# One matmul over both ends of a ring buffer: the fifth token tile of a fused attention and bilinear feed-forward kernel

## The chip, the cores and the metric

The kernel runs on one core of a Trainium2 chip. The metric is the device time of one execution in microseconds (us). The engines are named as in the profile: PE is TensorE's matrix multiplication and PEld its weight load, DVE is VectorE, ACT is ScalarE, POOL is GpSimd, SP is SyncE, which here only issues DMAs. A name with q behind it (SPq, POOLq) is that engine's instruction queue.

## The reference

Two stages, the second fed by the first. B is 8, H is 8, S is 576 and D is 64, so there are 4608 tokens of width 512; the hidden width is 1536.

```python
scores = np.matmul(q, k.transpose(0, 1, 3, 2)) / np.sqrt(D)
masks = [mask_local if h < H // 2 else mask_strided for h in range(H)]   # a band of 32, or every 32nd key
attn_out = softmax(np.where(masks, scores, -1e9)) @ v
x = attn_out.transpose(0, 2, 1, 3).reshape(B * S, H * D)
out = ((x @ w_a) * (x @ w_b)) @ w_out
```

## The kernel before, in words

**Tiles and slots.** The feed-forward part walks over nine tiles of 512 tokens, t = 0 to 8; the fifth tile is t = 4. A tile has sixteen slots, numbered 16 t + 0 to 16 t + 15. The first twelve (`ffn_ab`, f = 0 to 11) each make one block of 128 hidden columns: the projection a on four 128-row pieces of the width (kk = 0 to 3), then the projection b in the same way, each into a bank of PSUM (`ab_mm`, L617 to L627). ACT copies a into `a_sb` (L647) and DVE multiplies it by b into the tile `pf` (L650). The last four slots multiply `pf` by `w_out`. Tiles 2 to 8 do that with a seven-product scheme on pairs of token groups (`ffn_ys`, `y_plan`, L812), whose sums DVE makes ahead (`fast_s`, L758). For f = 0 the order of kk is 0 and 2, then 1, then 3 (L642), since pieces 1 and 3 of x come last.

**The attention of the next batches** is woven in. Each batch b has 576 tokens, and its steps stand in lists by slot (L584 to L592): S makes scores into a `st` bank (L392), then ACT's exponential and DVE's mask; V multiplies by v into an `o` bank (L470 or L529), after which either DVE normalizes into `xl` rows, or ACT takes a logarithm and an exponential (L538, L539) and DVE multiplies into xT (L545). `take(i)` runs the steps of slot i; `mid` runs those of slot i - 0.5 between a and b.

**The x ring.** xT holds the activations, transposed, in a ring of four batches: XR * S = 2304 columns (L160). Token n lies in column n modulo 2304. Tile t reads columns from 512 t modulo 2304 on. Only for t = 4 does that run over the end: tokens 2048 to 2303 are in columns 2048 to 2303, tokens 2304 to 2559 in columns 0 to 255. `ab_mm` cuts it there (`cuts`, L618 to L619): for t = 4 every projection is two matmuls of 256 columns, each with its own load of the same weights. For every other tile it is one of 512.

**PSUM banks.** The a and b banks and the three banks X, Y, Z of the output stage come from one pool of four (`mm_bank`, L612). A matmul into a bank waits until the engine that read its last content is done.

**SP's queue.** All DMAs of the later attention steps (L346, L350), the two halves of x that go through memory (`rows_out` L511 writes a scratch, `rows_in` L516 reads it back transposed into xT) and the stores of y leave through SP, in program order. `y_plan` stores its tile in two halves, i = 0 and 1, at slots 16 t + 19 and 16 t + 20, that is slots 3 and 4 of the next tile (L821, L822). Half i holds 128 partitions of two rows of 512 float32 values; a partition is (a, s) with a from 0 to 15 and s from 0 to 7, and the output row is 32 a + 16 i + 2 s + q (L806). Each DMA of SP also waits for the DMA that used the same of eight completion semaphores before it, which is the one eight places earlier on SP's queue. The buffers `y_sb` are two per tile, so the output stage of the next tile waits, before its first copy into each (L789), for the store that reads it.

The whole order on PE, DVE, ACT, POOL and SP is the program's own (`manual_schedule`, L905).

Of the kernel before, what the change touches and what calls it, by code (L numbers as in the profile page):

```python
# [31 lines left out]
def kernel(  # L32
# [10 lines left out]
    nc = tc.nc  # L43
    B, H, S, D = q.shape
# [7 lines left out]
    TTOK = 512  # L52
# [106 lines left out]
    XR = 4  # L159
    xT = const.tile([128, KD, XR * S], BF16)  # L160
# [5 lines left out]
    HT = TTOK // 2  # L166
# [437 lines left out]
    def take(pos):  # L604
        for b, names in steps.get(pos, ()):
            run(b, names)
# [5 lines left out]
    def mm_bank(shape):  # L612
        nm = "tp" if used[0] % 4 == 3 and used[0] >= 0 else "mm"
        used[0] += 1
        return psum4[nm].tile(shape, F32, tag=nm, name="mm")

    def ab_mm(t, f, ab, kks, mid=None, first=0, last=KD - 1, ws=(0, 1)):  # L617
        n = min(TTOK, XR * S - TTOK * t % (XR * S))  # L618
        cuts = [(0, n)] + ([(n, TTOK - n)] if n < TTOK else [])  # L619
        for w, ps_ in [((wa_sb, wb_sb)[i], ab[i]) for i in ws]:  # L620
            if mid and ps_ is ab[1]:
                mid()
            for kk in kks:
                for c0, n in cuts:
                    x0 = (TTOK * t + c0) % (XR * S)
                    nc.tensor.matmul(ps_[:, c0:c0 + n], lhsT=w[:, kk, 128 * f:128 * (f + 1)], rhs=xT[:, kk, x0:x0 + n],  # L626
                                     start=(kk == first and c0 == 0), stop=(kk == last and c0 == cuts[-1][0]))  # L627

    def ffn_ab(t, f, mid, ab=None):
        if f == 0:  # L630
            pfs[t] = fsb.tile([128, FD, TTOK], BF16, tag="pf", name="pf", bufs=1)
        pf = pfs[t]
        if f // 2 in FAST_A.get(t, ()):
            if f % 2 == 0:
                pairs[t, f // 2] = a_pair(t, f // 2)
            return next(pairs[t, f // 2])
        if ab is None:
            ab = [mm_bank([128, TTOK]) for _ in range(2)]
            if f == 0:

                late = 1 if t == 1 else 3
                for kks in ((0, 2, 3), (1,)) if t == 1 else ((0, 2), (1,), (3,)):  # L642
                    ab_mm(t, f, ab, kks, last=kks[-1] if kks[-1] == late else -1)
            else:
                ab_mm(t, f, ab, range(KD), mid)
        a_sb = fsb.tile([128, TTOK], F32, tag="a_sb", name="a_sb")
        nc.scalar.copy(a_sb, ab[0])  # L647
        if t in FAST_Y:
            halves = lambda x: x.rearrange("p (a i s) -> p a i s", i=2, s=16)
            nc.vector.tensor_mul(pf[:, f, :].rearrange("p (i a s) -> p a i s", i=2, s=16), halves(a_sb), halves(ab[1]))  # L650
        else:
            nc.vector.tensor_mul(pf[:, f, :], a_sb, ab[1])
        return pf[:1, f, :1]
# [109 lines left out]
    def products(t):  # L763
        pf, s = pfs[t], pss[t]
        full = lambda e, i: (lambda g, q: pf[:, 2 * g + e, HT * i + q:HT * (i + 1):2])
        summed = lambda n: (lambda g, q: s[:, n, g, q:HT:2])
        wsum = lambda n: (lambda g: wf[:, n, g])
        wfull = lambda e, j: (lambda g: wov[:, e, j, g])
        return {"1": ("X", full(0, 0), wfull(0, 0)), "2": ("Y", full(1, 0), wfull(1, 0)), "3": ("X", summed(3), wfull(1, 1)),
                "4": ("Z", full(1, 1), wsum(3)), "5": ("X", summed(0), wsum(0)), "6": ("X", summed(1), wsum(1)),  # L770
                "7": ("Z", summed(2), wsum(2))}
# [8 lines left out]
    def y_bufs():  # L780
        return [fsb.tile([128, 2, d_model], F32, tag="y_sb", name="y_sb", bufs=2) for _ in range(2)]

    def y_post(k, y, q, bank, n=slice(0, HN)):

        part = lambda i, j: y[i][:, q, HN * j:HN * (j + 1)]
        if k == "+":
            nc.vector.tensor_tensor(part(1, 1), part(1, 1), part(0, 1), op=ALU.add)  # L787
        elif k in "1765":
            nc.scalar.copy({"1": part(0, 0), "7": part(0, 1), "6": part(1, 0), "5": part(1, 1)}[k], bank)  # L789
        elif k == "4":  # L790
            nc.vector.tensor_tensor(part(1, 0), bank, part(1, 0), op=ALU.add)
        elif k == "2":
            nc.vector.tensor_tensor(y[0][:, q, n], bank, y[0][:, q, n], op=ALU.add)
        elif k == "3":
            nc.scalar.copy(part(0, 1), bank)
# [4 lines left out]
    def y_plan(t):  # L800

        plan, y = products(t), y_bufs()
        bank = {x: mm_bank([128, 2, HN]) for x in "ZXY"}

        def store_half(i):
            rows = out[TTOK * t:TTOK * (t + 1)].rearrange("(a i s q) c -> a s i (q c)", i=2, s=8, q=2)  # L806
            nc.sync.dma_start(out=rows[:, :, i], in_=y[i].rearrange("p q c -> p (q c)"))

        for n, (k, q) in enumerate(Y_ORDER):
            b, lhs, rhs = plan[k]  # L810
            for g in range(FG):
                nc.tensor.matmul(bank[b][:, q], lhsT=lhs(g, q), rhs=rhs(g), start=k in "172" and q == 0 and g == 0,  # L812
                                 stop=g == FG - 1, skip_group_check=True)
                if g == FG - 1:
                    if q == 1:
                        y_post(k, y, slice(0, 2), bank[b])
                        if k == "5":
                            y_post("+", y, slice(0, 2), None)
                    take(("y", t, n + 1))
                yield y  # L820
        do(16 * t + 19, store_half, 0)  # L821
        do(16 * t + 20, store_half, 1)  # L822
# [82 lines left out]
    with tc.manual_schedule(engines={ENG.PE, ENG.SP, ENG.Pool, ENG.DVE, ENG.Activation}):  # L905
# [11 lines left out]
        for x, src in ((raw[0], k), (raw[1], q)):  # L917
            nc.sync.dma_start(out=x[:96].rearrange("p (h r d) -> p h r d", h=2, d=D),
                              in_=src[0, 0:2].rearrange("h (p r) d -> p h r d", r=RL))
# [15 lines left out]
        first = {}  # L935
        for nm in ORDER:
            if nm[0] == "*":
                spin(int(nm[1:]))
            elif nm == "C0":
                for x, cp, n in ((raw[0], nc.vector.tensor_copy, "k"), (raw[1], nc.scalar.copy, "q")):  # L940
                    t = nats[0, n, False][:, 0:2].rearrange("p h r d -> p (h r d)")
# [5 lines left out]
            elif nm == "M":  # L947
                mask_local2()
            elif nm[0] == "G":
                mask_group(int(nm[1]))  # L950
                if nm == "G1":
                    load_vs(0)
                    for c in range(2):
                        load_w(c)
                    load_w(2)
                    load_qk(1, True, (0, 1))
                    load_qk(1, True, (2, 3))
                    load_vs(1)
                    load_w(3)
                    load_qk(1, False)  # L960
            elif nm == "Z":
                zero_qz(1, nc.scalar, ((0, 0),))
            elif nm[0] == "F":
                f = int(nm[1])
                if nm[2] == "A":
                    if f == 1:
                        ab = pst.tile([128, 2, 512], F32, tag="st", name="ab")
                        first[f] = [ab[:, 0], ab[:, 1]]
                    else:
                        first[f] = [psum4["misc"].tile([128, 512], F32, tag="misc", name="ab")]  # L970
                elif nm == "F0B":
                    first[f].append(psum4["o"].tile([128, 512], F32, tag="o", name="ab"))
                ab_mm(0, f, first[f], {"A": (0, 1), "B": (0, 1), "b": (2,), "c": (3,)}[nm[2]],
                      ws={"A": (0,), "B": (1,)}.get(nm[2], (0, 1)))
            else:
                PART[nm[:-2] + nm[-1]](int(nm[-2]))
# [15 lines left out]
        def do(i, fn, *args):  # L992
            at.setdefault(i, []).append(lambda: fn(*args))
# [99 lines left out]
```

## Time and profile before

| what | value |
|---|---|
| three runs | 325.45, 325.69, 326.91 us; median 325.69 |
| the profiled execution | 325.6 us, of which the span from first to last instruction is 323.9 |
| busy: PE, DVE, ACT, POOL | 317.7, 258.6, 189.4, 161.0 us |
| granted TensorE clock | 1.000 |
| tile 4, from its first matmul to the first of its output stage | 159.49 to 183.47 us |
| tile 5, the same | 193.66 to 217.13 us |

A busy time counts every moment with an instruction of that engine under way. A matmul's recorded duration is longer than the distance to the next one, since matmuls overlap in the array; so distances between starts tell the cost, and durations do not. "Idle before" is the time that an engine stood still ahead of a group, with the releaser that ended most of it. The chain that ended last walks back from the last instruction: at each step to whatever released it, or else to the instruction before it on its engine.

### The profile page before, as it was taken

To read this page: it belongs to the slowest core of one execution; us is meant where nothing else is said; L and a number is where in the kernel's file an instruction comes from. 1 tells how busy PE (TensorE), PEld (TensorE's weight loads), DVE (VectorE), ACT (ScalarE), POOL (GpSimd) and SP (SyncE) were. 2 spreads that over 40 slices of the span, in tenths; PEclk is the share of its full clock that TensorE was granted. 3 is DMA by queue.
4 is the path that set the end of the run, shared out by engine and by line. 5 is a ranking of instruction groups with operands and counts; after the bars stand their busy time and mean duration, and the time that the engine had idled before them with its cause. 6 is when DMAs were issued, how large, how long until landed. Compare 5 with 4: busy or idle time off the path is not lost.

```text
span 323.9 us, 7466 instructions
## 1 busy us (share of the span) xinstructions
PE 317.7 (98%) x2686; PEld 209.2 (65%) x2686; DVE 258.6 (80%) x560; ACT 189.4 (58%) x332; POOL 161.0 (50%) x291
## 2 busy tenths in 40 slices
PE   8999999999999999999999999999999999999994
PEld 6754655455555587557999885569555966686673
DVE  6766888888778899898888888988999768837952
ACT  6764775478764576447644764476546655335541
POOL 8935848599857554853576247634013012203500
PEclk9999999999999999999999999999999999999999
DMA  9999999999999989999999999999146040004004
GB/s 158 151 203 194 204 187 188 170 174 129 141 216 142 134 87 98 111 209 152 101 101 189 176 97 106 175 194 115 33 95 157 10 130 3 0 0 132 1 2 130
DMA packets 110724, 40.43 MB, mean 125 GB/s; under 512 B 88672, under 2 KB 107744, under 8 KB 110688
## 3 DMA queue, kind: packets, MB, share of 16 engines
q0 software_dynamic: 85968, 19.48, 67.0%
q1 hardware_dynamic: 24576, 20.42, 25.1%
q8 instruction: 21, 0.34, 0.5%
q14 instruction: 15, 0.12, 0.1%
q10 hardware_dynamic: 144, 0.07, 0.1%
HBM read 39.51 MB, written 10.91 MB: 156 GB/s over the span
## 4 chain that ended last, share of the span: by engine, by line
PE 95%; DMA 1%; ACT 1%; DVE 1%; issue 0%; SPq 0%
PE mm L626 46%; PE mm L812 17%; PE mm L876 6%; PE mm L710 5%; PE st L392 4%; PE o L470 2%; PE ax L703 2%; PE o L529 2%; PE mm L703 2%; PE mm L841 2%; PE end L841 1%; DMA raw<-in_q_dram 1%; PE misc L155 1%; PE ab L626 1%; PE tp L296 1%; PE tp L554 1%
## 5 line engine op out<-in xcount | busy, mean ns | idle before, releaser
L626 PE MATMUL mm<-xT,wa_sb 128*128 128x512 bf16 (+1 forms) x400 | 92.6, 353 | 0.0
L626 PE MATMUL mm<-xT,wb_sb 128*128 128x512 bf16 (+1 forms) x400 | 92.6, 353 | 0.0
L647 ACT COPY a_sb<-mm 128x512 f32<-128x512 f32 x88 | 51.4, 585 | 51.3 <-PE mm L626 49.3
L626 PEld LDWEIGHTS <-wb_sb 128*128 128x128 bf16 x408 | 39.4, 98 | 35.6 <-DMA wb_sb<-in_moe_w_b_dram 0.2
L1059 POOL CAST pace<-pf 1x1 f32<-1x1 bf16 x83 | 24.7, 298 | 69.0 <-DVE pf L650 48.3
L626 PEld LDWEIGHTS <-wa_sb 128*128 128x128 bf16 x408 | 36.6, 98 | 23.1 <-issue 0.2
L650 DVE TENSOR_TENSOR pf<-a_sb,mm 128x512 bf16<-128x512 f32 x66 | 44.8, 680 | 8.4 <-PE mm L626 7.2
L413 ACT ACTIVATE p<-st 72x576 bf16<-72x576 f32 (+1 forms) x56 | 36.4, 650 | 14.4 <-PE st L392 14.2
L545 DVE TENSOR_TENSOR xT<-o,xr 64x288 bf16<-64x288 f32 x48 | 21.4, 446 | 14.7 <-ACT xr L539 14.4
L812 PEld LDWEIGHTS <-ps 128*128 128x128 bf16 x288 | 28.0, 98 | 3.1
L789 ACT COPY y_sb<-mm 128x512 f32<-128x512 f32 (+1 forms) x28 | 15.5, 555 | 17.9 <-PE mm L812 15.3
L812 PE MATMUL mm<-wf,ps 128*128 128x256 bf16 x216 | 25.5, 273 | 0.0
L538 ACT ACTIVATE xr<-o 64x576 f32<-64x576 f32 x28 | 18.1, 647 | 12.0 <-PE o L529 11.7
L876 PE MATMUL mm<-wo_sb,pf 128*128 128x512 bf16 x96 | 23.4, 379 | 0.0
L243 POOL DMA_DIRECT2D vs<-in_v_dram x24 | 19.6, 818 | 5.0 <-PE mm L812 2.4
L812 PEld LDWEIGHTS <-pf 128*128 128x128 bf16 x216 | 20.3, 98 | 2.5 <-issue 0.2
L1059 POOL COPY pace<-y_sb 1x1 f32<-1x1 f32 x23 | 5.0, 217 | 33.2 <-DVE y_sb L787 19.8
L710 PE MATMUL mm<-xT,wb_sb 128*128 128x512 bf16 x72 | 21.4, 379 | 0.0
L539 ACT ACTIVATE xr<-xr 64x576 f32<-64x576 f32 x28 | 19.1, 683 | 0.9
L812 PE MATMUL mm<-wo_sb,pf 128*128 128x256 bf16 x144 | 18.5, 273 | 0.1
L212 POOL DMA_DIRECT2D kl<-in_k_dram x24 | 16.1, 672 | 4.8 <-issue 3.2
L212 POOL DMA_DIRECT2D ql<-in_q_dram x24 | 15.9, 664 | 5.0 <-DMA wo_sb<-in_moe_w_out_dram 3.9
(189 smaller groups left out, 574.4 us busy)
## 6 DMA issues: line engine op xcount, KB each, us to landing
out_dram<-y_sb SPq DMA_DIRECT2D x12, 512.0 KB, 5.0
out_dram<-y_sb SPq DMA_DIRECT2D x11, 256.0 KB, 3.6
vl<-in_v_dram POOLq DMA_DIRECT2D x6, 384.0 KB, 8.2
kl<-in_k_dram POOLq DMA_DIRECT2D x24, 72.0 KB, 3.3
ql<-in_q_dram POOLq DMA_DIRECT2D x24, 72.0 KB, 3.3
vs<-in_v_dram POOLq DMA_DIRECT2D x24, 72.0 KB, 4.3
wo_sb<-in_moe_w_out_dram POOLq DMA_DIRECT2D x4, 384.0 KB, 9.2
natk<-in_k_dram POOLq DMA_DIRECT2D x20, 72.0 KB, 3.5
```

The source lines that it names most:

```text
L212: nc.gpsimd.dma_start(out=t[32 * h:32 * h + 32], in_=src[b, h].rearrange("(i y) d -> y i d", y=32))
L243: nc.gpsimd.dma_start(out=vs_buf[b % 2][:, h, :, 0:D], in_=v[b, HL + h].rearrange("(p r) d -> p r d", r=RS))
L413: nc.scalar.activation(p_flat(p)[:M, :2 * W].rearrange("p (i n) -> p i n", n=2 * n), st[:M].rearrange("p a (i n) -> p (a i) n", n=256)[:, ...
L539: nc.scalar.activation(r, r, ACT.Exp, scale=-1.0)
L545: nc.vector.tensor_mul(dst.rearrange("d (p r) -> d p r", r=RS)[:, :, G * half:G * (half + 1)], o[:64, j, :W].rearrange("d (g p) -> d p g", ...
L626: nc.tensor.matmul(ps_[:, c0:c0 + n], lhsT=w[:, kk, 128 * f:128 * (f + 1)], rhs=xT[:, kk, x0:x0 + n], start=(kk == first and c0 == 0), sto ...
L647: nc.scalar.copy(a_sb, ab[0])
L650: nc.vector.tensor_mul(pf[:, f, :].rearrange("p (i a s) -> p a i s", i=2, s=16), halves(a_sb), halves(ab[1]))
L710: nc.tensor.matmul(got[e], lhsT=wb_sb[:, kk, 128 * f:128 * (f + 1)], rhs=xT[:, kk, x0:x0 + TTOK], start=kk == 0, stop=kk == KD - 1)
L812: nc.tensor.matmul(bank[b][:, q], lhsT=lhs(g, q), rhs=rhs(g), start=k in "172" and q == 0 and g == 0, stop=g == FG - 1, skip_group_check=True)
L876: nc.tensor.matmul(ybank[j], lhsT=pf[:, f, 128 * j:128 * (j + 1)], rhs=wo_sb[:, f], start=(f == 0), stop=(f == FD - 1))
L1059: nc.gpsimd.tensor_copy(pace, done)
```

## The change

The fifth tile's two cuts become one operand. The ring is seen as nine pieces of 256 columns, and a step of eight takes the first and the last: columns 0 to 255, then 2048 to 2303. One matmul of 512 columns reads both. The tokens then stand in `a`, `b`, `pf` and y with their halves swapped, so that partition (a, s) of y holds token group a + 8 or a - 8; the store puts that right by writing each half of y in two DMAs of 64 partitions, each to the other half of the rows. That makes four stores of 256 KB for this tile in the place of two of 512 KB. No other tile changes.

```diff
+    x_wraps = lambda t: TTOK * t % (XR * S) + TTOK > XR * S
+
+    def x_tile(t, kk):
+
+        if x_wraps(t):
+            return xT[:, kk].rearrange("p (z m) -> p z m", m=HT)[:, ::XR * S // HT - 1]
+        x0 = TTOK * t % (XR * S)
+        return xT[:, kk, x0:x0 + TTOK]
+
     def ab_mm(t, f, ab, kks, mid=None, first=0, last=KD - 1, ws=(0, 1)):
-        n = min(TTOK, XR * S - TTOK * t % (XR * S))
-        cuts = [(0, n)] + ([(n, TTOK - n)] if n < TTOK else [])
         for w, ps_ in [((wa_sb, wb_sb)[i], ab[i]) for i in ws]:
             if mid and ps_ is ab[1]:
                 mid()
             for kk in kks:
-                for c0, n in cuts:
-                    x0 = (TTOK * t + c0) % (XR * S)
-                    nc.tensor.matmul(ps_[:, c0:c0 + n], lhsT=w[:, kk, 128 * f:128 * (f + 1)], rhs=xT[:, kk, x0:x0 + n],
-                                     start=(kk == first and c0 == 0), stop=(kk == last and c0 == cuts[-1][0]))
+                nc.tensor.matmul(ps_, lhsT=w[:, kk, 128 * f:128 * (f + 1)], rhs=x_tile(t, kk), start=kk == first,
+                                 stop=kk == last)
...
         def store_half(i):
             rows = out[TTOK * t:TTOK * (t + 1)].rearrange("(a i s q) c -> a s i (q c)", i=2, s=8, q=2)
-            nc.sync.dma_start(out=rows[:, :, i], in_=y[i].rearrange("p q c -> p (q c)"))
+            if not x_wraps(t):
+                nc.sync.dma_start(out=rows[:, :, i], in_=y[i].rearrange("p q c -> p (q c)"))
+                return
+            for z in range(2):
+                nc.sync.dma_start(out=rows[8 - 8 * z:16 - 8 * z, :, i],
+                                  in_=y[i][64 * z:64 * z + 64].rearrange("p q c -> p (q c)"))
```

## The prediction

> **What bounds the kernel.** I read the page's parts 1 and 4 first, then PE's waits, the three neighbouring tiles as windows, the chain through the fifth tile, and SP's timeline where that tile's stores leave.
>
> ```profile
> PE 317.7 (98%) x2686; PEld 209.2 (65%) x2686; DVE 258.6 (80%) x560; ACT 189.4 (58%) x332; POOL 161.0 (50%) x291
> ...
> PE 95%; DMA 1%; ACT 1%; DVE 1%; issue 0%; SPq 0%
> ```
>
> PE carries 95% of the chain that ended last. PE's waits by name are two in the whole trace, 0.9 and 0.4 us, both early. So a saving counts if it shortens PE's sequence, and only there. How much can it be? The windows of the fourth, fifth and sixth tile, each from its first score matmul to that of the next tile (columns: length, then busy time and count of PE, PEld, DVE, ACT, POOL, the granted clock, DMA share, GB/s):
>
> ```profile
> 125.57:159.24 33.67, 33.67 (x266) 21.36 (x264) 29.55 (x61) 20.16 (x33) 19.01 (x37) 1.00 1.11 143
> 159.24:193.42 34.18, 34.07 (x363) 30.81 (x361) 29.58 (x61) 20.16 (x33) 18.82 (x37) 1.00 1.19 140
> 193.42:227.09 33.67, 33.67 (x267) 21.36 (x265) 29.52 (x61) 20.16 (x33) 19.15 (x37) 1.00 1.23 143
> ```
>
> The tiles on both sides do the same work without the cut, and take 33.67 us each. The fifth takes 34.18, although it loads weights for 9.45 us more (30.81 against 21.36). So those loads lie almost wholly beside matmuls, and all that is special about the fifth tile is **0.51 us**. The 0.11 us between 34.18 and its busy 34.07 shows a stall, and hides part of it, as the end of the matmul before it is drawn out past the next one's start. The chain through its end (start, us, what) names it:
>
> ```profile
> 179.10 0.28 PE o L529 x8
> ...
> 179.39 0.66 ACT xr L538
> ...
> 180.07 0.69 ACT xr L539
> ...
> 180.79 0.38 DVE xT L545
> ...
> 182.82 0.61 DVE pf L650
> ...
> 183.47 1.47 PE mm L812 x12
> ```
>
> The chain leaves PE behind slot f = 9, runs through ACT, DVE's writes of x, two DVE steps left out here, and the `pf` of f = 10 back to PE at the output stage's first matmul: its bank was f = 10's, and is free once that `pf` has been read. The last two blocks of projections are off the chain.
>
> **Part by part.**
>
> *The merged matmuls.* 96 pairs of 256 columns (12 slots by 2 projections by 4 kk) become 96 matmuls of 512. The price is the distance between starts. From PE's timeline:
>
> ```profile
> 159.49 0.60 PE L626 MATMUL mm<-xT,wa_sb 128*128 128x256 bf16 x4
> ...
> 178.93 0.42 PE L529 MATMUL o<-p,vs 72*128 72x72 bf16 x8
> ...
> 182.94 0.42 PE L529 MATMUL o<-p,vs 72*128 72x72 bf16 x8
> ```
> ```profile
> 193.66 0.59 PE L626 MATMUL mm<-xT,wa_sb 128*128 128x512 bf16 x2
> ...
> 212.91 0.42 PE L529 MATMUL o<-p,vs 72*128 72x72 bf16 x8
> ...
> 216.87 0.42 PE L529 MATMUL o<-p,vs 72*128 72x72 bf16 x8
> ```
>
> The first fence is the fifth tile, the second the sixth, with the same attention steps between. Twelve slots take 182.94 - 159.49 = 23.45 against 216.87 - 193.66 = 23.21 us: **0.24 us** for 96 pairs, 2.5 ns each. Ten slots, to the V step that feeds the chain, take 19.44 against 19.25: **0.19 us**.
>
> *The price of reading two pieces.* No projection reads two distant pieces before, so I bound it. The score matmuls L392 do: their moving operand is two pieces of 96 columns, from two planes of one buffer, and three of them stand 0.25 us apart from what follows, some 82 ns each. In the chain, blocks of single-piece matmuls take 1.75 us for 16 of 256 columns and 1.73 us for 8 of 512: 109.4 and 216.2 ns, that is 0.417 ns a column and 2.5 ns a matmul, or 82.6 ns for 192 columns. So the second piece costs nothing there; below nothing has no reason. At the other end a piece could cost what a matmul's fixed part costs, 2.5 ns, and the whole gain is gone. I take nothing.
>
> *The stall.* PE is ready for the output stage at 182.94 + 0.26 = 183.20 (216.87 to 217.13 in the sixth tile) and starts at 183.47: 0.27 us. With 0.24 of the cut that is the 0.51. After the change PE is ready 0.24 earlier, but the chain that it waits for starts 0.19 earlier. The program's order of instructions and waits keeps that wait on f = 10's `pf`. The stall is then 0.27 + 0.24 - 0.19 = 0.32, and the net gain is **0.19 us**. One bank is handed out differently: the b of f = 9 takes the bank of f = 8's a and not that of f = 7's b. Its reader, ACT's copy, ends at 176.85 in ACT's timeline and the matmul starts at 178.06, so 1.2 us of cover hides it; without it PE would wait for what is missing.
>
> *The stores.* Two issues more on SP, each some 0.6 us:
>
> ```profile
> 207.35 0.60 SPq L807 DMA_DIRECT2D out_dram<-y_sb  x1
> 208.00 2.73 SPq L516 DMA_TRANSPOSE xT<-xd  x1
> 210.78 0.60 SPq L807 DMA_DIRECT2D out_dram<-y_sb  x1
> 211.50 3.06 SPq L346 DMA_DIRECT2D kT1l<-tk  x2
> ...
> 220.61 1.16 SPq L516 DMA_TRANSPOSE xT<-xd  x1
> ```
>
> Queued behind the first extra store is the read-back of x at 208.00. It takes 2.73 us where the next takes 1.16, so it waits about 1.6 us for its scratch, which hides 0.6. Behind the second is the pair of `kT1l`, 3.06 us where the next such pair takes 1.17: 1.9 us of waiting hide 0.6. PE sees nothing of either. If both covers were gone, SP would be 1.2 us late at the read-back of 220.61. Its landing time in this stretch is 5.1 to 6.3 us, so at worst it lands at 226.9; its first reader is PE's kk = 1 at 228.20. Cover is 1.3 us.
>
> *How soon the halves land* is not in the trace: no store of 64 partitions is. The nearest rows are the same halves as one DMA, 4.0 to 5.8 us (median 5.0), and 256 KB stores of 128 partitions at 3.6 us. Best case 3.6; worst case each half takes as long as the whole and they follow each other, 10 to 11.6 us. I take 5.0. Waiting for them: the sixth tile's copies into `y_sb` at 218.72 and 221.56, and the read-back at 220.61, which stands eight places behind the last store and so waits for it. Seen from the second pair's issue at 210.78, that is 9.8 us, plus 1.3 of cover: nothing reaches PE up to 11.1 us.
>
> The rule that speaks against this part is in the Trainium skill, "DMA: Bandwidth & Descriptors", section "Why a DMA increments its semaphore by 16 and not by 1": the number of DMA engines is the largest up to 16 that divides the slowest dimension of both sides. The new store's output side has 8 there (16 before), so by the rule each runs on 8 engines. By it a pair would land in twice the old time, an estimate of 10 us, at 220.8: the read-back would start 0.2 us late, inside its cover, and the sum would still be 0.19 us, but what is left before the late-store rival below begins is 1.1 us in place of 6.1. No run here shows it.
>
> **The sum.** 0.19 us off the profiled execution's 325.6 gives 325.4. That execution lies 0.09 under the median of the runs, 325.69; the forecast for the median is 325.69 - 0.19 = **325.5 us**.
>
> **Rivals.**
> - *The stall goes too.* If f = 10's `pf` came earlier, the fifth tile would be like its neighbours: -0.51, 325.2 us. For: neither neighbour has the stall. Against: the wait is still in the program, and the DVE and ACT work ahead of it is untouched.
> - *No gain.* Two distant pieces cost 2.5 ns a matmul, or twice that: 0 to +0.24, 325.7 to 325.9 us. Against: L392.
> - *The weight loads were in the way.* 96 loads of 98 ns are 9.4 us; 316 us. Against: the windows, which leave 0.51 us for everything.
> - *Slower: the stores land late.* SP stands at the read-back of 220.61, the transposed x comes late, and PE waits at the seventh tile's kk = 1. It decides from a landing of 11.1 us of the second pair on; beyond that each us is one of the total. At three times the 5.0 us, 15, it costs 3.9 - 0.2: 329.4 us. For: the DMA share is above 1.1 through these tiles and the software queue takes 74% of 16 engines in 205 to 225 us. Against: twice the old time still fits.
>
> **How the numbers follow.** Forecast 0.74, the stall gone 0.08, no gain 0.12, loads 0.02, late stores 0.04. Half a per cent, about what a measurement of this kernel can tell from no change, is 1.6 us; the first three cases lie within it, so faster 0.02, same 0.94, slower 0.04. The range takes the first three cases, 325.2 to 325.9, and 0.2 us either way, the distance between the two lower runs: 325.0 to 326.1.
>
> **What would show it.** Right: the fifth tile's window falls from 34.18 to 33.99, its twelve slots from 23.45 to 23.21, and the first output matmul still follows DVE's `pf`, 0.3 us after PE was ready. PEld's busy time falls by some 9 us and the span by 0.2. Wrong: the merged matmuls stand further apart than 216 ns, the window reaches 33.67, or PE idles at the start of the seventh tile behind the read-back of x.

## The result and the profile after

The median of 22 runs of the changed kernel is 327.10 us (326.00 to 328.88); that of the kernel before, now over 22 runs, is 326.44 us (325.45 to 331.39). The ratio is 1.0028 with an interval of 1.0016 to 1.0040: slower by 0.9 us, 0.5 to 1.3. (The ratio leaves out one slow run of the kernel before, 331.39 us, which the medians hold.) The forecast was 325.5 us with a range to 326.1. So it missed by 1.6 us, of two parts: 0.75 us is the median of the kernel before, which three runs had put at 325.69; the rest is the change, +0.66 by medians where -0.19 was forecast.

The profiled execution took 326.57 us with a span of 324.9. Busy times and the shares of the chain of waits, as the page gives them:

```profile
PE 316.5 (97%) x2561; PEld 200.5 (62%) x2590; DVE 258.8 (80%) x560; ACT 189.6 (58%) x332; POOL 161.9 (50%) x291
...
PE 87%; DMA 4%; POOL 4%; DVE 1%; issue 1%; ACT 1%; POOLq 0%; DVEq 0%
```

PEld fell by 96 loads and 8.7 us, and nothing came of that, as forecast. (Of PE's matmuls 29 records are missing here, so its busy time is not compared.) DMA and POOL in the chain belong to the start of the program, where one and the same program differs from run to run by over 1 us, as the first experiment shows. Below, I therefore compare lengths of windows and not clock times.

The fourth, fifth and sixth tile, each from its first score matmul to that of the next (columns as in the prediction):

```profile
125.98:159.65 33.67, 33.51 (x263) 21.36 (x264) 29.55 (x61) 20.18 (x33) 19.09 (x37) 1.00 1.22 140
159.65:193.63 33.98, 33.83 (x267) 21.39 (x265) 29.54 (x61) 20.18 (x33) 19.19 (x37) 1.00 1.21 142
193.63:227.30 33.67, 33.51 (x264) 21.35 (x265) 29.52 (x61) 20.18 (x33) 19.22 (x37) 1.00 1.16 142
```

The fifth takes 33.98 us; 33.99 was forecast, after 34.18. So the saving of 0.20 us is there, and the loss lies elsewhere. SP's timeline where the tile's stores leave is the first place to look (start, us, and what; x2 are the two stores of a half):

```profile
207.58 1.47 SPq L816 DMA_DIRECT2D out_dram<-y_sb  x2
209.09 3.46 SPq L516 DMA_TRANSPOSE xT<-xd  x1
212.60 1.24 SPq L816 DMA_DIRECT2D out_dram<-y_sb  x2
214.31 3.50 SPq L346 DMA_DIRECT2D kT1l<-tk  x2
...
222.41 1.58 SPq L516 DMA_TRANSPOSE xT<-xd  x1
```

The second half's stores leave at 212.60 and 213.23, not at 210.78. By their completion records the four land 5.1, 6.1, 6.8 and 8.2 us after their issue, the last at 221.45, while ACT's first copy into that buffer starts at 221.77: nothing waits in this execution, by 0.3 us.

The other place is the end. The program's last DVE step, as the chain has it (start, us, what), and SP's waits at the end of its list, here called closing waits, for stores to land (us in total, times, longest), first of the kernel before:

```profile
319.33 0.29 DVE y_sb L793
```
```profile
SPq L1088 <- DMA out_dram<-y_sb: 1.9, 1, 1.9
```

and of the changed one:

```profile
319.55 0.29 DVE y_sb L798
```
```profile
SPq L1098 <- DMA out_dram<-y_sb: 2.9, 3, 1.3
```

From that step to the end of the span it is 323.9 - 319.33 = 4.6 us before, and 324.9 - 319.55 = 5.35 after: **0.75 us more at the end of the program**, in code that the diff doesn't touch. The DMA view of the last microseconds, after the change and before it (q14 is a queue whose packets the trace calls instruction; the last lines are the last stores of y, with their landing times):

```profile
q14 instruction: 1, 0.01, 1.2%
...
out_dram<-y_sb SPq DMA_DIRECT2D x1, 64.0 KB, 3.6
```
```profile
out_dram<-y_sb ACTq DMA_DIRECT2D x1, 64.0 KB, 2.8
out_dram<-y_sb SPq DMA_DIRECT2D x1, 64.0 KB, 2.5
```

After the change the last store lands in 3.6 us in place of 2.5, and a fetch of 8 KB of code runs beside it. In its records 15 of that store's 16 completions come at 322.29 to 322.55 and the sixteenth at 323.63; the fetch starts at 322.15. Before, the last fetch on this queue starts at 324.21, behind the store and 0.3 us behind the program's last instruction.

The records of the single packets say more. The store is 128 packets of 512 bytes. After the change 120 of them are through before the fetch starts; the other eight, a sixteenth, start where the fetch ends, at 322.64.

### The profile page after: what moved, and what is told of

Read it like the earlier page. It is cut to its first block, busy times and chain, and to the rows that moved or that the text cites. A ratio compares the mean times of both kernels' runs of the same rounds, so it can differ in the third digit from the quotient of the medians.

```text
span 324.9 us, 7248 instructions
## 1 busy us (share of the span) xinstructions
PE 316.5 (97%) x2561; PEld 200.5 (62%) x2590; DVE 258.8 (80%) x560; ACT 189.6 (58%) x332; POOL 161.9 (50%) x291
## 4 chain that ended last, share of the span: by engine, by line
PE 87%; DMA 4%; POOL 4%; DVE 1%; issue 1%; ACT 1%; POOLq 0%; DVEq 0%
PE mm L631 44%; PE mm L822 17%; PE mm L886 6%; PE st L392 4%; DMA wb_sb<-in_moe_w_b_dram 4%; PE mm L715 4%; PE ax L708 2%; PE o L529 2%; PE mm L708 2%; PE o L470 2%; PE mm L851 2%; POOL shared L197 1%; PE end L851 1%; POOL vl L225 1%; POOL wa_sb L252 1%
## 5 line engine op out<-in xcount | busy, mean ns | idle before, releaser
L631 PE MATMUL mm<-xT,wb_sb 128*128 128x512 bf16 x349 | 92.1, 379 | 0.4
L631 PE MATMUL mm<-xT,wa_sb 128*128 128x512 bf16 x335 | 90.6, 379 | 1.0 <-DVE a_sb L741 0.2
L631 PEld LDWEIGHTS <-wb_sb 128*128 128x128 bf16 x360 | 34.7, 98 | 40.5 <-DMA wb_sb<-in_moe_w_b_dram 0.6
L655 DVE TENSOR_TENSOR pf<-a_sb,mm 128x512 bf16<-128x512 f32 x66 | 44.9, 680 | 8.2 <-PE mm L631 7.0
L631 PEld LDWEIGHTS <-wa_sb 128*128 128x128 bf16 x360 | 31.9, 98 | 25.2 <-issue 0.2
L538 ACT ACTIVATE xr<-o 64x576 f32<-64x576 f32 x28 | 18.1, 648 | 11.9 <-PE o L529 11.6
L715 PE MATMUL mm<-xT,wb_sb 128*128 128x512 bf16 x67 | 20.5, 379 | 0.1
L657 DVE TENSOR_TENSOR pf<-a_sb,mm 128x512 bf16<-128x512 f32 x22 | 14.9, 677 | 4.6 <-ACT a_sb L652 2.7
```

What stands on the lines that cost most here:

```text
L538: nc.scalar.activation(r, sums, ACT.Ln)
L631: nc.tensor.matmul(ps_, lhsT=w[:, kk, 128 * f:128 * (f + 1)], rhs=x_tile(t, kk), start=kk == first, stop=kk == last)
L715: nc.tensor.matmul(got[e], lhsT=wb_sb[:, kk, 128 * f:128 * (f + 1)], rhs=xT[:, kk, x0:x0 + TTOK], start=kk == 0, stop=kk == KD - 1)
```

## The experiments

These theories stood against each other in the course of it; the expectations use their letters. S: the four stores cost the time. M: the merged matmuls do. P: the program as a whole does, outside the fifth tile. N: identical programs differ by as much. E: stores of 64 partitions run on half as many DMA engines, land late and hold up ACT's copy into the buffer. C: two DMAs more on SP are enough for that stall. F: the mere number of SP's DMAs moves the last code fetch beside the last store. Where an edit is shown without the lines that leave other tiles as they were, a comment in it names the tiles.

### The kernel before, once more

No edit.

> The kernel before, unchanged, as its own rival: what two identical programs differ by. Theory P (the change does in the fifth tile what was forecast, and the loss is made by the program as a whole, outside that tile: start, weight loads, last store): ratio 1.000, interval no wider than 0.002 either way. Theory S (the four stores cost it) and theory M (the merged matmuls cost it) expect the same. Theory N (the measurement differs by this much between identical programs): a ratio off by 0.2% or more.

Measured: 1.0004 (0.9992 to 1.0016). Its profile has a span of 325.3 us, 1.4 more than the other one, and PE is 1.33 us later from 82.84 us on and stays so to the end. So the time before the fifth tile differs by over 1 us between executions of one program, and the ratio over many runs is what counts. At the end it is 4.6 us, as before.

### The stores alone

The kernel before with its cut projections, and the fifth tile's halves stored in two DMAs of 64 partitions each:

```diff
-            nc.sync.dma_start(out=rows[:, :, i], in_=y[i].rearrange("p q c -> p (q c)"))
+            for z in range(2):      # t == 4
+                nc.sync.dma_start(out=rows[8 * z:8 * z + 8, :, i],
+                                  in_=y[i][64 * z:64 * z + 64].rearrange("p q c -> p (q c)"))
```

> The fifth tile keeps its two cuts; its two stores become four of 64 partitions, to the rows that they belong to. Theory S: about +0.9 us, ratio 1.003, and its trace shows the fifth tile's window still at 34.18 us and a later tile longer. Theory P: the fifth tile's and all later windows as before; the ratio may be anywhere within 0.3% of 1, since this is again another program. Theory M: 1.000. If each store runs on fewer DMA engines, a half lands in more than 5 us, some 8 to 10 for the pair.

Measured: 1.0036 (1.0023 to 1.0048), 1.2 us. The stores alone cost what the change costs and somewhat more. The chain through the sixth tile's output stage in this kernel (start, us, what):

```profile
209.54 3.44 SPq L516
...
213.03 0.59 SPq L811
...
213.67 9.91 DMA out_dram<-y_sb
...
223.73 0.59 ACT y_sb L789
...
224.37 1.49 PE mm L817 x12
```

The last of the four stores is issued at 213.67 and lands 9.9 us later; ACT's copy into the buffer that it reads waits for it, and PE for ACT's bank. By the starts of PE's groups, PE loses 1.00 us here against the kernel before. ACT's waits name another DMA for the same 2.1 us, `qz1l<-tq`; the chain and the completions, the last at 223.58, name the store. The end takes 326.4 - 321.19 = 5.2 us. In this execution the two places add up to 1.65 us, more than the 1.2 of the ratio, so the wait need not be as long in every run.

### The merged matmuls alone

The change's `x_tile` and `ab_mm` with the two stores of before, so that the fifth tile's rows leave with their halves swapped:

```diff
-            if not x_wraps(t):
-                nc.sync.dma_start(out=rows[:, :, i], in_=y[i].rearrange("p q c -> p (q c)"))
-                return
-            for z in range(2):
-                ...
+            nc.sync.dma_start(out=rows[:, :, i], in_=y[i].rearrange("p q c -> p (q c)"))
```

> The merged matmuls alone; the fifth tile's two stores stay as before, so its rows leave with their halves swapped in the output. Theory S: -0.19 us, ratio 0.9994. Theory M: about +0.9 us, ratio 1.003. Theory P: the fifth tile's window at 33.99 us as in the changed kernel, all later tiles as before, and a ratio that the start and the end decide.

Measured: 1.0002 (0.9987 to 1.0016). PE gains 0.2 us over the fifth tile, as in the change, and the end is that of before: last store 2.5 us, one closing wait. The loss is not in the matmuls.

### The change, once more

No edit.

> The changed kernel again. All theories but N: ratio 1.0028 within 0.0015. N: it may come out at 1.000. Theory P: the fifth tile's window again 33.98 us and the sixth to ninth as before, with the difference to the kernel before split between the time ahead of the third tile and the time behind the last matmul.

Measured: 1.0032 (1.0012 to 1.0052). Its profile has the end's 5.4 us and the fetch beside the last store again. It also has a short wait in the sixth tile, 1.23 us of ACT for the store, which PE feels as 0.18:

```profile
222.51 0.59 ACT L794 COPY y_sb<-mm 128x512 f32<-128x512 f32 x1 [1.23 <-DMA out_dram<-y_sb]
```

The four stores land here in 4.7, 5.8, 7.9 and 8.9 us. So the sixth tile stands right at the edge: 221.45 was early enough, 222.36 is not.

### Four stores of 128 partitions

The kernel before, with the fifth tile's halves cut by the row parity q, and not by partitions: as many DMAs and bytes as in the change, but each over all 128 partitions.

```diff
-            nc.sync.dma_start(out=rows[:, :, i], in_=y[i].rearrange("p q c -> p (q c)"))
+            for q in range(2):      # t == 4
+                y_store(nc.sync, t, y, i, q)
```

> The kernel before, with the fifth tile's two stores made four in another way: by the parity q of the row, so each has 128 partitions and an outermost dimension of 16, and 256 KB as in the change. Theory E (a store whose outermost dimension is 8 runs on 8 of the 16 DMA engines, lands late and holds up the sixth tile's output stage): no stall in the sixth tile, each store with 16 completions. Theory C (two DMAs more on SP are enough for that stall): the sixth tile's output stage stalls by up to 1 us as in the stores alone. Theory F (two DMAs more on SP bring the last fetch of its code from behind the program's last store to beside it, and one of that store's 16 completions comes 1 us late): the last store lands in 3.5 us and not 2.5, and the time is +0.75 us, ratio 1.0023. E and F together: 1.0023; C and F: 1.0036; E without F: 1.000.

Measured: 1.0025 (1.0011 to 1.0039), 0.8 us. These stores land in 4.2 to 5.2 us, nothing waits in the sixth tile, and the end costs 325.0 - 319.54 = 5.5 us, with the fetch at 322.18 and the last store at 3.7 us. The last store, in the DMA view of the end:

```profile
out_dram<-y_sb SPq DMA_DIRECT2D x1, 64.0 KB, 3.7
```

So this kernel has the end's cost by itself, and the late landing belongs to the cut by partitions and not to the number of stores. That cut makes two things smaller at once, the partitions of a store (128 to 64) and its outermost dimension (16 to 8); no run here separates them.

### The change and eight DMAs more than before

The change, with the stores of tiles 2, 3 and 5 cut by q as well. SP then has eight DMAs more than before, and since there are eight completion semaphores, the last store is back on the one that it had:

```diff
+            if t in (2, 3, 5):
+                for q in range(2):
+                    y_store(nc.sync, t, y, i, q)
+                return
```

> The changed kernel, with the two stores of the third, fourth and sixth tile cut by row parity: six DMAs more on SP, eight more than before, none of them with fewer than 128 partitions. Theory F: the last fetch of SP's code comes well before the last store, which lands in 2.5 us again; what remains is -0.19 us of the merged matmuls and 0 to 1 us of the sixth tile's stall: ratio 1.0005, between 0.9994 and 1.002. Without F (each DMA more costs by itself): above 1.0032, by eight DMAs over two some 1.01.

Measured: 0.9998 (0.9984 to 1.0012). With six more DMAs the change's loss is gone. The fetch starts at 316.1, before the last store is issued at 320.25; by its completions that store takes 2.5 us, and the end is 324.1 - 319.77 = 4.3. SP closes with one wait for a store again:

```profile
SPq L1102 <- DMA out_dram<-y_sb: 1.8, 1, 1.8
```

The fifth tile's stores still land late here (the last in 8.3 us, at 221.21), in time by a little.

### The step taken backwards

The ring read in the tokens' order, so that no rows are swapped and two stores do:

```diff
-            return xT[:, kk].rearrange("p (z m) -> p z m", m=HT)[:, ::XR * S // HT - 1]
+            return xT[:, kk].rearrange("p (z m) -> p z m", m=HT)[:, ::1 - XR * S // HT]
```

> The merged matmul reads the two ends of the ring in the order of the tokens, by a step backwards over the pieces, so nothing is swapped and the stores are those of the kernel before. Nothing is left of E and F: the fifth tile's window at 33.98 us, the end as before, -0.19 us, ratio 0.9994. If a step backwards costs the read something, the twelve slots take more than 23.21 us.

Measured: 0.9992 (0.9974 to 1.0009); run once more beside a later kernel, 0.9998 (0.9980 to 1.0016):

> The merged matmuls with the step taken backwards (the pieces in the order of the tokens) and two stores, a second time, as the base for the next kernel: PE's sequence is 0.2 us shorter, the end as before, ratio 0.9994.

Both profiles show PE's 0.2 us and the end of before (4.6 us). One reading of the ring backwards does what the swapped rows and four stores were for; that it is faster than before is not shown by the times, since both intervals hold 1.

### Stores of 32 partitions

The kernel before, with each half of the fifth tile in four stores of 32 partitions:

```diff
-            nc.sync.dma_start(out=rows[:, :, i], in_=y[i].rearrange("p q c -> p (q c)"))
+            for z in range(4):      # t == 4
+                nc.sync.dma_start(out=rows[4 * z:4 * z + 4, :, i],
+                                  in_=y[i][32 * z:32 * z + 32].rearrange("p q c -> p (q c)"))
```

> The kernel before, with each of the fifth tile's stores cut into four of 32 partitions, outermost dimension 4. Theory E, a larger dose: 4 engines, each half some 12 us of transfers (512 KB took 3 of its 5.0 us for them on 16), the second half behind the first, so it lands some 24 us after the first issue, 10 us after the sixth tile wants its buffer: 6 to 11 us, ratio 1.02 to 1.035. Theory C: six DMAs more cost what two do, times three at most: under 4 us.

Measured, over four runs: 1.0147 (1.0127 to 1.0166), 4.8 us; the direction is the theory's, the size is under what was expected, because the stores overlap: the last of them lands at 224.93, after 8 to 9 us each in the second half. ACT and PE wait (total, times, longest; ACT's wait again bears the name of another DMA, but its copy starts at 225.03, 0.1 us behind that landing):

```profile
ACT y_sb L789 <- DMA qz1l<-tq: 4.3, 1, 4.3
...
PE mm L817 <- ACT y_sb L789: 2.7, 1, 2.7
```

By its starts PE is 4.4 us later behind this place. A store of 128 partitions has 16 completion records, one of 64 has 9 and one of 32 has 5. Of the 9 and of the 5, one comes ahead of all others, 1.0 to 3.8 us after the issue; 8 and 4 are left for the data, which fits theory E's 8 and 4 engines. So with the cut by partitions fewer completions carry a store, and it lands later. SP's closing waits are 2.7 us in four, and the fetch is beside the last store again.

### Ten DMAs more

In both the kernel before and the one with eight more DMAs the last store is on the first semaphore that SP waits for at the end. So it was open whether the order of those waits starts the fetch, or SP's place in its list of instructions. Ten more DMAs put the last store on the semaphore that it has in the change, and SP's place still further off. All of them have 128 partitions: the stores of tiles 2 to 6 are cut by q:

```diff
-            nc.sync.dma_start(out=rows[:, :, i], in_=y[i].rearrange("p q c -> p (q c)"))
+            for q in range(2):      # t <= 6
+                y_store(nc.sync, t, y, i, q)
```

> The kernel before, with both halves of tiles 2 to 6 stored by row parity: ten DMAs of SP more, all of 128 partitions. Ten is two more than eight, so the last store stands on the same completion semaphore as in the change, but SP's list of instructions is longer by five times as much. Order theory: in the change SP's closing waits pass two semaphores before the last store's own, SP so gets further in its list, and that starts the code fetch beside the last store. Then the last 64 KB store takes 3.6 us again, SP closes with three waits, and the ratio is 1.0023 (+0.75 us). Count theory: the fetch stands at a fixed place of the list, and with ten more DMAs SP passes it long before the last store, as with eight more. Then the store takes 2.5 us and the ratio is 1.000. Under both nothing stalls in the sixth tile beyond 0.2 us, since all of these stores land in 4 to 5 us.

Measured: 0.9989 (0.9974 to 1.0004). SP's closing waits and the last store in this kernel:

```profile
SPq L1092 <- DMA out_dram<-y_sb: 1.8, 3, 1.3
```
```profile
out_dram<-y_sb SPq DMA_DIRECT2D x1, 64.0 KB, 2.5
```

There are three waits, as in the change, and no cost: the fetch is at 316.2, the store takes 2.5 us, and the end 324.2 - 319.95 = 4.25. So the closing waits ahead of the last store's own do not bring the cost by themselves, and the order theory falls in the form that was on record; the count theory's forecast came true. Its fixed place in the list does not hold, though. In the five profiles with the cost SP stands at the closing wait next ahead of the last store's own, or is just through it, as the fetch starts, and in the list of these waits that is four places later with six DMAs more than with two. A fixed place would be passed earlier with six. So the number of DMAs decides, and how it sets the fetch's place is open.

### Another bank for the first output matmul

The fifth tile's remaining 0.3 us is the first output matmul's wait for the bank of f = 10's b. On top of the backward step, the three banks of the fifth tile's output stage are handed out in another order:

```diff
-        bank = {x: mm_bank([128, 2, HN]) for x in "ZXY"}
+        bank = {x: mm_bank([128, 2, HN]) for x in ("XZY" if t == 4 else "ZXY")}
```

> The backward step, and for the fifth tile the banks of the output stage handed out as X, Z, Y in place of Z, X, Y: the first output matmul then takes the bank of f = 10's a, which ACT has read long before, and the bank of f = 10's b goes to the second product, 1.5 us later. Bank theory: the bank is all that the first output matmul waits for; the stall of 0.3 us goes, the fifth tile's window is 33.67 us as its neighbours', 0.5 us in all, ratio 0.9984. Rival: what the first product multiplies comes late as well, and the stall stays at 0.2 to 0.3 us behind another releaser: ratio 0.9994, as the kernel beside it.

Measured: 0.9989 (0.9972 to 1.0006). The fifth tile took 33.67 us, as its neighbours. But in the sixth tile the first b, which follows its a by 0.43 us in the kernel before and in the backward step without this, follows by 0.59:

```profile
194.32 0.59 PE L631 MATMUL mm<-xT,wa_sb 128*128 128x512 bf16 x2
194.91 0.59 PE L631 MATMUL mm<-xT,wb_sb 128*128 128x512 bf16 x2
```

Its bank was X's, and ACT's last copy out of X ended at 194.86. So 0.16 of the 0.51 us were lost again.

The order Z, Y, X gives the first product the bank of f = 11's a and leaves Z's for the sixth tile:

```diff
+        bank = {x: mm_bank([128, 2, HN]) for x in ("ZYX" if t == 4 else "ZXY")}
```

> The same with the banks of the fifth tile's output stage handed out as Z, Y, X: X, which the first product and the last one use, takes the bank of f = 11's a, whose copy by ACT ended at 183.06 in the trace of the backward step, 0.33 us before PE is ready; and the bank that goes on to the sixth tile's first b is again Z's, read early. In the kernel with X, Z, Y that bank was X's, whose last copy by ACT ended at 194.86, and the sixth tile's b started 0.16 us late. If that is so, the fifth tile takes 33.67 us, the 0.16 us do not come back, and PE is 0.51 us ahead of the kernel before through the sixth tile: ratio 0.9984. Rival: another bank's reader is late there, the sixth tile's first slots lose 0.1 us or more, and the ratio is 0.999.

Measured: 0.9987 (0.9975 to 0.9999): the interval leaves out 1, if only by 0.0001, and it is one of a dozen intervals. The kernel was not run beside the one with X, Z, Y. The fifth tile in it:

```profile
159.91:193.58 33.67, 33.67 (x266) 21.36 (x264) 29.51 (x61) 20.16 (x33) 19.11 (x37) 1.00 1.12 143
```

By the starts of PE's groups it is 0.67 us later than the kernel before ahead of the fifth tile and 0.17 behind it, and that stays so through the sixth: 0.50 us. 0.0013 of 326 is 0.4.

## Why the prediction was wrong

**The matmuls: right.** PE's timeline at both ends of the twelve slots, after the change:

```profile
159.90 0.59 PE L631 MATMUL mm<-xT,wa_sb 128*128 128x512 bf16 x2
...
183.11 0.43 PE L529 MATMUL o<-p,vs 72*128 72x72 bf16 x8
```

They took 183.11 - 159.90 = 23.21 us as forecast, the two distant pieces cost nothing, and the window came out at 33.98 against 33.99. The weight loads went for nothing, and the rival of 316 us fell.

**The stall: right.** The chain through the fifth tile's end after the change:

```profile
179.31 0.28 PE o L529 x8
...
183.03 0.61 DVE pf L655
183.64 0.04 issue
183.68 1.36 PE mm L822 x11
```

PE was ready at 183.11 + 0.26 = 183.37 and started at 183.68: 0.31 us, 0.32 was forecast, behind the same `pf`. The last two experiments show that the bank was all of it.

**The stores: the step that failed.** "Two issues more on SP" were costed at nothing ("PE sees nothing of either"), so the sum held the 0.19 us of the matmuls and no term against it. Three things were wrong in that.

*The cover was not there.* "It takes 2.73 us where the next takes 1.16, so it waits about 1.6 us for its scratch, which hides 0.6": the scratch's write had landed at 206.34 by its completions, 1.7 us before that read-back was issued at 208.00. The row was long for another reason, which stays open (2.4 to 3.5 us in the kernels with whole or 64-partition stores ahead of it, 1.6 to 1.7 behind stores cut by q). So the extra issue pushed it, and the second pair left at 212.60 and 213.23 in place of the 210.78 from which the cover of 11.1 us was counted: 2.4 us of that were gone (0.2 of them since this execution reaches the tile's stores that much later). The `kT1l` pair's 1.9 us hid nothing either: that pair ended 3.2 us later (217.81 for 214.56).

*The landing and its waiter.* 5.0 us were taken, with 3.6 to 11.6 as bounds; the last store of the four took 8.2 to 9.9 us in the three profiles with these stores and no others added. The rule of the Trainium skill, "DMA: Bandwidth & Descriptors", section "Why a DMA increments its semaphore by 16 and not by 1", gives 8 engines for these stores, by their outermost dimension. The trace agrees: 9 completions against 16, of which one comes ahead of the data. By it a pair lands in an estimated 10 us; from a second pair's first issue to its last landing the three profiles have 8.85 to 10.55. The prediction had this estimate beside the sum and not in it, which put the landing too early. Who would wait was wrong as well: the read-back at 222.41 came in time for PE, while ACT's copy into the buffer, which the prediction lists and did not carry further, comes first. It cost PE nothing in one profile of the change, 0.18 us in the other, and 1.00 with the stores alone, where PE reaches it later but the stores land later still.

*The end of the program.* This is the larger term, and no step of the prediction had it. With two more DMAs on SP the last code fetch falls beside the program's last store, which lands 1.1 us later and ends the program 0.75 us later. Of the fourteen profiles, the five with two or six DMAs more (four kernels) have the fetch there, and ends of 5.1 to 5.5 us. The seven with none have it behind the end, and ends of 4.5 to 4.6. The two with eight and ten more have it ahead of the last store, and ends of 4.2 to 4.3. So the cost comes with the number of DMAs, and not with the matmuls or the kind of store; it goes away again when there are more. That the fetch holds up the sixteenth completion is read from the packets, since no run moves the fetch alone: in all five profiles the store's last eight packets start within 0.01 us of the fetch's end, and the other 120 are through before it starts. Of these eight the last four or five took 59 to 102 ns in place of 27, and why is open. The trace does not say on which DMA engine they ran.

**The sum.** -0.20 for the matmuls, +0.75 at the end, and 0 to 0.18 for the wait behind ACT's copy make 0.55 to 0.73 us. The ratio of 1.0028 says 0.9, with 0.5 to 1.3 in its interval. How often ACT waits, and how long, in the runs without a profile is not known.

**The rivals and chances.** "The stores land late" was the right suspicion at 0.04, with the wrong waiter and a price near 4 us; stores of 32 partitions cost 4.8, those of the change under 0.2 in the two profiles. Within 0.5% had 0.94, and that is where the result lies, since half a per cent is 1.6 us; but it was given to a gain or to nothing, and the result is a loss. The range was too narrow for two more reasons. It hung on a median of three runs, which 19 more moved by 0.75 us: 0.19 off the later median, 326.25 us, lies above it as well. And it was drawn from the first three cases, so a slower kernel had no place in it.

## What to carry to other kernels

Before a transfer is cut, ask along which side: cut by partitions, which here made the outermost dimension smaller too, the stores had 9 or 5 completions and landed later; cut by columns of a partition, they had all 16 and landed as before. Hold the buffer's next writer, and not only the queue behind the store, against the landing time. A long row of a queue is not a wait, unless what it waits for is shown to come later. And a few DMAs more may cost time far from the edit: compare the last store's landing and the closing waits first, when a kernel is slower by less than a microsecond and its loops are not.

## What the runs showed of the hardware

- Landing of the fifth tile's halves, each 512 KB in all: in two stores of 128 partitions 4.7 to 6.7 us (seven profiles), in four of 128 partitions 4.2 to 6.0 (two), in four of 64 partitions 4.7 to 9.9 (four), in eight of 32 partitions 3.9 to 9.2 (one).
- A code fetch of 8 KB beside a store of 64 KB: the store lands in 3.5 to 3.7 us and not 2.5, through one of its sixteen completions. Its last eight packets start where the fetch ends.
- A moving operand of two pieces of 256 columns costs what one of 512 does, forwards and backwards: 23.21 to 23.22 us for the twelve slots, and 23.21 in a tile without it.
- A wait for a PSUM bank moves with the order in which banks are handed out: 0.31 us with Z, X, Y, 0.16 us in the next tile with X, Z, Y, and nothing with Z, Y, X.
